# Opening and second batch of an attention-and-mixer kernel: feature widths, head halves, engines and slots changed

## Chip, core and metric

The kernel runs on one core of one Trainium2 chip. A core has TensorE (PE in the profile, with PEld for the loading of its weights), VectorE (DVE), ScalarE (ACT), GpSimd (POOL) and SyncE (SP), each with its own queue of instructions taken in order, and DMA queues filled by some of them. PE writes to PSUM, whose tiles here come from two pools. The metric is the device time of one execution in microseconds (us), compared as a median of runs.

## What is computed

Linear attention with cosine and sine weights of the position, and then a mixer over tokens and over channels. Shapes: batch B = 8, heads H = 8, sequence S = 576, head size D = 64, so a row has 512 columns after the heads are joined.

```python
def phi(x, c, s):
    r = np.maximum(x, 0.0)
    return np.concatenate([r * c, r * s], axis=-1)
q_p = phi(q, cos_w, sin_w)
k_p = phi(k, cos_w, sin_w)
kv = np.einsum('bhsf,bhsd->bhfd', k_p, v)
z = np.sum(k_p, axis=2)
num = np.einsum('bhsf,bhfd->bhsd', q_p, kv)
den = np.einsum('bhsf,bhf->bhs', q_p, z)[..., None] + 1e-06
x = num / den                       # heads joined: [B, 576, 512]
h = np.maximum(x.T @ w_tok1, 0.0) @ w_tok2      # over tokens: 576 -> 256 -> 576
u = x + h.T
h2 = np.maximum(u @ w_ch1, 0.0) @ w_ch2         # over channels: 512 -> 1536 -> 512
out = u + h2
```

## The kernel before

The sequence is cut into four blocks of 128 rows (0 to 3) and a tail of 64 rows that the code calls block R (R = 4); the tail holds four heads in each half of the partitions. The features of one block, cosine and sine side by side, have 128 columns for each head, so each head of a block is one 128x128 tile. For each batch there are two stages.

The **front** (class `Front`) makes u. `feature` (L210) computes relu and weight in one instruction on DVE (L227) or ACT (L225); `k_side` and `q_side` call it for cosine and sine. `ksum` (L239) adds up key features on PE, `ksum_out` copies the sums on ACT, `dens` multiplies query features by them. `q_trans` (L301) turns the query features of a block on PE, eight heads into one PSUM tile, and copies them out on ACT or DVE into `qpT`. `values` casts v into `v_aug`. `kv` (L273) multiplies keys by values into `kv_ps`, `kv_out` copies it to `kv_sb`. `num` (L320) multiplies turned queries by `kv_sb` and DVE divides into `x_sb`. `tok1`, `tok1_out` and `tok2` are the token mixer; `tok2` writes u with one addition on DVE for each block, `u_ps` being its PSUM tile.

The **channel** stage (class `Channel`) has 12 steps of the first product (`c_main`, with `c_tail` for the tail rows behind it) and then steps of the second (`o_step`, two matmuls of 512 columns each, for the first batch in 26 steps: the blocks 0 and 1 in turn, 12 steps; block 2, 6 steps; R, 2; block 3, 6). A finished block is added to u on DVE and stored by a DMA from SP.

The channel stage of a batch carries the front of the next one. `pieces` (L449) returns a plan, a slot number for each piece; slot C + n follows step n, slot O + n follows step 12 + n, and slot -1 comes before the first step. What a slot issues stands on each engine's queue behind the step, in the order of the plan. For the first batch the steps 0 to 2 are empty, since `first_front` has done their products. The second batch's u is turned by two transposing DMAs on SP (`u_trans_dma`, L421), which `c_main` of the second batch waits for. `tok2` of the first batch stands in slots too, for u is not needed until the first `o_step` ends.

The very first front (`first_front`, L593) has nothing to hide behind. It runs on loads that are cut into head halves: the low heads 0 to 3 of q, k and v come from one DMA each, the high heads from another; that of q's high heads is issued by ACT, all others by SP. Between its products stand fillers, `busy` (L184): matmuls of 512 columns of zeros into `idle_ps`, in PE's order like any other instruction. In this front u is made turned, straight from x and the token weights (`turned_x`, `turned_b`), and the first three steps of the channel product follow (`c_block`, L507).

PSUM: pool `ps_mm` has four buffers of one bank, pool `ps_at` two of two banks. The program gives a tile a buffer that is free in program order; the tile's first matmul then waits until the last reader of the buffer's earlier tile is done. All orders are written out by hand; the engines run in that order.

Loads of the later batches are issued by SP in `load_batch`: the second batch's behind the first channel weights, the third batch's behind the second channel weights.

Of the kernel before, what the change touches and what calls it, by code (L numbers as in the profile page):

```python
# [9 lines left out]
F32 = mybir.dt.float32  # L10
BF16 = mybir.dt.bfloat16
# [5 lines left out]
def kernel(  # L17
# [15 lines left out]
    nc = tc.nc  # L33

    B, H, S, D = q.shape
# [4 lines left out]
    P = 128  # L40
    R = S // P
    SM = R * P
    ST = S - SM
    NSC = R + 1
    NCC = Dm // P
    NT = D_tok // P
    NCH = D_ch // P
    HH = H // 2
# [8 lines left out]
    def half(g):  # L57
        return slice(g * ST, (g + 1) * ST)
# [12 lines left out]
    ps_mm = ctx.enter_context(tc.tile_pool(name="ps_mm", bufs=4, space=bass.MemoryType.PSUM))  # L71
    ps_at = ctx.enter_context(tc.tile_pool(name="ps_at", bufs=2, space=bass.MemoryType.PSUM))
# [111 lines left out]
    def busy(dst, times):  # L184
        for _i in range(times):
            nc.tensor.matmul(dst, ident, zeros[:, 0:dst.shape[-1]], start=True, stop=True)  # L186
# [10 lines left out]
    class Front:  # L197
# [100 lines left out]
                     self.kv_ps[g][:, 0:HH * DP]  # L298
                     .rearrange("p (j d) -> p j d", d=DP)[:, :, 0:D1])

        def q_trans(self, ci, heads=(0, H), eng=nc.scalar):  # L301
            lo, hi = heads if ci < R or self.padded else (0, HH)
            if hi - lo == H:
                qT_ps = ps_at.tile([P, H, P], BF16, name="qT_ps", tag="at")
            else:
                qT_ps = ps_mm.tile([P, HH, P], BF16, name="qT_ps", tag="mm")
            for h in range(lo, hi):
                nc.tensor.transpose(qT_ps[:, h - lo, :],  # L308
                                    self.qp[ci][:, h, :, :].rearrange("p a b -> p (a b)"), ident)
            dst = self.qpT[:, ci * H + lo:ci * H + hi, :]  # L310
            if eng is nc.scalar:
                nc.scalar.copy(dst, qT_ps)  # L312
            else:
                nc.vector.tensor_copy(dst, qT_ps)
# [3 lines left out]
                                        in_=self.qp[ci].rearrange("p h a b -> p (h a b)"))  # L318

        def num(self, ci, fill=0, dens=False):  # L320
            num_ps = ps_at.tile([P, 2, 512], F32, name="num_ps", tag="at")
            if fill:
                busy(num_ps[:, 0, HH * DP:512], 1)
            n = 2 if ci < R else 1
            for h in range(H):
                g, j = divmod(h, HH) if ci < R else (h % 2, h // 2)
                kv = self.kv_sb[g][:, j, 0:D1]
                cols = slice(j * DP, j * DP + D1)
                if ci < R:
                    nc.tensor.matmul(num_ps[:, g, cols], self.qpT[:, ci * H + h, :], kv,  # L330
                                     start=True, stop=True)
                elif self.padded:
                    nc.tensor.matmul(num_ps[:, 0, cols], self.qpT[:, R * H + g * HH + j, :], kv,
                                     start=(g == 0), stop=(g == 1))
                else:
                    nc.tensor.matmul(num_ps[half(g), 0, cols], self.qpT[:, R * H + j, half(g)], kv,
                                     start=True, stop=True)
            nv = num_ps[:, 0:n, 0:HH * DP].rearrange("p g (j d) -> p g j d", d=DP)
            if dens:
                den = self.d_sb[:, ci * H:ci * H + n * HH, :].rearrange("p (g j) o -> p g j o", g=n)  # L340
            else:
                den = small.tile([P, 2, HH, 1], F32, name="den")[:, 0:n]
                nc.vector.tensor_scalar_add(den, nv[:, :, :, D:D1], 1e-6)  # L343
                nc.vector.reciprocal(den, den)
            nc.vector.tensor_mul(  # L345
                self.x[:, ci, 0:n * DH].rearrange("p (g j d) -> p g j d", g=n, j=HH),
                nv[:, :, :, 0:D], den.to_broadcast([P, n, HH, D]))
# [101 lines left out]
        def pieces(self, first=False):  # L449


            V, KV, N = self.values, self.kv, self.num
            KS, QS, QT, T = self.k_side, self.q_side, self.q_trans, self.tok2
            C, O = 0, NCH
            if first:

                plan = [(C + at, KS, ci, 0 < ci < R) for ci, at in enumerate((3, 4, 5, 5, 6))]
                plan += [(C + at, QS, ci) for ci, at in enumerate((6, 7, 8, 8, 9))]
                plan += [(C + at, QT, ci, (0, H), nc.vector if ci == R else nc.scalar)
                         for ci, at in enumerate((9, 10, 11, 12, 13))]  # L460
                plan += [(C + at, V, ci, nc.vector) for ci, at in enumerate((10, 11, 11, 11, 11))]
                plan += [(O + at, KV, ci) for ci, at in enumerate((1, 1, 1, 2, 2))]
                plan.append((O + 2, self.kv_out, (0, 1), nc.vector))
            else:
                plan = [(C + at, V, ci, nc.scalar) for ci, at in enumerate((-1, -1, 0, 1, 2))]
                plan += [(C + at, KS, ci) for ci, at in enumerate((0, 0, 1, 2, 2))]
                for ci, at in zip(ORDER, (1, 2, 3, 4, 5)):
                    plan += [(C + at, QS, ci), (C + at, self.q_trans_dma, ci)]
                plan += [(C + at, KV, ci) for ci, at in enumerate((2, 3, 4, 6, 7))]
                plan.append((C + 8, self.kv_out))  # L470
            if first:
                at, mix, t = (O + 4, O + 6, O + 7, O + 9, O + 10), O + 11, O + 14
            else:
                at, mix, t = (C + 9, C + 10, C + 11, O + 1, O + 3), O + 4, O + 8
            plan += [(i, N, ci) for i, ci in zip(at, ORDER)]
            plan += [(mix, self.mix_head, 0), (mix + 1, self.mix_head, 1),
                     (mix + 2, self.mix_tail)]

            plan += [(t + at, T, ci) for ci, at in enumerate((0, 1, 2, 3, 3))]
            plan += [(t + 2, self.u_trans_dma, 0, 3), (t + 3, self.u_trans_dma, 3, NSC)]  # L480
            slots = {}
            for slot, what, *args in sorted(plan, key=lambda p: p[0]):
                slots.setdefault(slot, []).append((what, args))
            return slots


    AHEAD = 3
# [105 lines left out]
    def first_front(f):  # L593


        idle_ps = ps_at.tile([P, 2, 512], F32, name="idle_ps", tag="at")[:, 0, :]
        lo_heads, hi_heads = (0, HH), (HH, H)
        busy(idle_ps, 12)

        for j in range(2):  # L600
            f.feature("q", 3, j, lo_heads, on_act=True)
        for heads in (lo_heads, hi_heads):
            for ci in range(R):
                if (heads, ci) != (lo_heads, 3):
                    f.feature("q", ci, 0, heads)
                    f.feature("q", ci, 1, heads)
                f.q_trans(ci, heads)
                busy(idle_ps, 1)
        f.q_side(R)
        f.q_trans(R)  # L610
        busy(idle_ps, 2)
        for ci in range(R):
            f.feature("k", ci, 0)
            f.feature("k", ci, 1, on_act=(ci > 1))
            busy(idle_ps, 2)
            f.ksum(ci)
        f.k_side(R)
        busy(idle_ps, 2)
        f.ksum(R)
        busy(idle_ps, 1)  # L620
        for ci in range(R):
            if ci == 2:
                f.ksum_out()
            f.values(ci, nc.scalar, lo_heads)
        cast_tok1(0)
        f.values(R, nc.vector)
        for ci in range(R):
            f.values(ci, nc.vector, hi_heads)
        for ci in (0, 1, 2):
            f.dens(ci)  # L630
        for ci in range(NSC):
# [64 lines left out]
    w_ch2_done = load_w_ch2(done[1])  # L696
    f = Front(0, results[0])
    c = first_front(f)
    for b in range(B):
        slots = Front(b + 1, results[b + 1]).pieces(first=(b == 0)) if b + 1 < B else {}  # L700
        if b == 0:
            for ci in range(NSC):
                slots.setdefault(AHEAD + ci, []).insert(0, (f.tok2, (ci, ps_at, False)))
        if b > 0:
            c = Channel(b, results[b])
        for what, args in slots.pop(-1, ()):
            what(*args)
        for i, step in enumerate(c.steps(AHEAD if b == 0 else 0)):
            step()
            for what, args in slots.pop(i, ()):  # L710
                what(*args)


            if b == 0 and i == NCH:
                load_batch(2, "kvq", behind=w_ch2_done[1])
            if 0 < b < B - 2 and i == NSC:
                load_batch(b + 2, "vq")
            if b < B - 3 and i == NCH + (18 if b == 0 else 12):
                load_batch(b + 3, "k")
        assert not slots  # L720
# [32 lines left out]
```

## Time and profile before

| what | us |
|---|---|
| median of 3 runs | 274.07 (273.32 to 274.42) |
| the profiled execution, its own time | 273.47 |
| its span, first to last instruction | 271.7 |
| PE busy | 262.8 (97% of the span) |
| DVE busy | 165.4 (61%) |
| ACT busy | 123.8 (46%) |
| PE's first matmul of `c_block` (end of the first front) | 24.94 |
| last `o_step` matmul of the first batch ends, second batch's first product starts | 60.87, 61.81 |
| one batch in the middle, from `c_main` to `c_main` | 30.4 |

A row of the timeline reads: start in us, length in us, engine, line, operation, the tile written and the tiles read, shape, count of instructions merged into the row, and in brackets the idle time before it with what ended it. The length of a PE row runs to the end of its last matmul, which overlaps the next, so what a row costs PE is read from its start to the next start. A row of the waits reads: who waited, for whom, us in total, times, longest. Some records of matmuls can be missing from a trace.

### The profile page before, as it was taken

Reading aid. Unit: us, or ns where it says so; the run is one execution under the profiler, and the core shown is the slowest. Engines: PE = TensorE matmul, PEld = TensorE weight load, DVE = VectorE, ACT = ScalarE, POOL = GpSimd, SP = SyncE. Lnnn points to the kernel's source line nnn. Section 1 sums busy time; section 2 is a strip of 40 time slices with the busy share of each in tenths; the row PEclk is TensorE's granted clock in tenths of the full one; section 3 lists DMA queues with packets and bytes.
Section 4 is the critical chain, followed back from the end, with each engine's and each line's share of the span. In section 5 each row is a group of like instructions: output and inputs, shape, how many; then the busy total and the mean of one; then the engine's idle time right before and its main releaser. Section 6 shows DMA issues by size and latency. Waiting matters only on the chain.

```text
span 271.7 us, 5917 instructions
## 1 busy us (share of the span) xinstructions
PE 262.8 (97%) x2386; PEld 145.5 (54%) x2414; DVE 165.4 (61%) x421; ACT 123.8 (46%) x235; POOL 7.8 (3%) x21
## 2 busy tenths in 40 slices
PE   7989999999999999999999999999999999999994
PEld 2566466445555456455555455455555455454542
DVE  4954696759466495649666596639666586630031
ACT  4963882055616264236616264236625364315500
POOL 3400300000000000000000000000000000000000
PEclk9999999999999999999999999999999999999999
DMA  7999999959994889868696988769795453061022
GB/s 214 371 258 300 318 189 274 355 65 297 198 321 91 240 228 215 278 161 275 134 281 186 281 165 237 243 159 278 156 325 137 151 117 80 39 183 41 0 80 97
DMA packets 95483, 54.46 MB, mean 200 GB/s; under 512 B 62688, under 2 KB 90976, under 8 KB 95456
## 3 DMA queue, kind: packets, MB, share of 16 engines
q1 hardware_dynamic: 92016, 50.28, 66.7%
q0 software_dynamic: 2832, 3.21, 7.1%
q10 hardware_dynamic: 608, 0.59, 0.7%
q8 instruction: 19, 0.31, 0.5%
q14 instruction: 8, 0.07, 0.1%
HBM read 35.85 MB, written 9.44 MB: 167 GB/s over the span
## 4 chain that ended last, share of the span: by engine, by line
PE 92%; ACT 3%; DMA 2%; DVE 1%; issue 1%; POOL 0%; POOLq 0%; ACTq 0%
PE o_ps L535 29%; PE c_ps L501 29%; PE b_ps L358 5%; PE u_ps L386 4%; PE ct_ps L520 4%; PE kv_ps L287 4%; PE idle_ps L186 3%; PE o_ps L539 3%; PE num_ps L330 3%; DMA uT<-u_bf 2%; ACT qpT L312 1%; PE b_ps L362 1%; PE c_ps L511 1%; PE u_ps L390 1%; PE qT_ps L308 1%
## 5 line engine op out<-in xcount | busy, mean ns | idle before, releaser
L535 PE MATMUL o_ps<-w_ch,h1T 128*128 128x512 bf16 x367 | 94.1, 379 | 1.2
L501 PE MATMUL c_ps<-uT,w_ch 128*128 128x512 bf16 (+2 forms) x384 | 92.2, 372 | 1.0 <-DMA uT<-u_bf 0.9
L505 ACT ACTIVATE h1T<-c_ps 128x512 bf16<-128x512 f32 x93 | 55.7, 601 | 62.6 <-PE c_ps L501 62.4
L545 DVE TENSOR_TENSOR o_sb<-o_ps,u_sb 128x512 f32<-128x512 f32 (+1 forms) x40 | 25.4, 635 | 53.1 <-PE o_ps L535 49.6
L535 PEld LDWEIGHTS <-h1T 128*128 128x128 bf16 x384 | 35.1, 98 | 35.6 <-issue 1.6
L501 PEld LDWEIGHTS <-w_ch 128*128 128x128 bf16 x384 | 32.5, 97 | 29.2 <-DMA uT<-u_bf 1.4
L520 PEld LDWEIGHTS <-w_ch 128*128 128x128 bf16 x384 | 22.0, 98 | 18.4
L393 DVE TENSOR_TENSOR u_sb<-u_ps,x_sb 128x512 f32<-128x512 f32 (+1 forms) x40 | 24.7, 633 | 9.8 <-PE u_ps L386 9.5
L395 ACT CAST u_bf<-u_sb 128x512 bf16<-128x512 f32 (+1 forms) x35 | 19.4, 574 | 18.5 <-DVE u_sb L393 16.9
L520 PE MATMUL ct_ps<-uT,w_ch 128*128 128x64 bf16 x384 | 24.1, 193 | 0.0
L368 ACT ACTIVATE B<-b_ps 128x512 bf16<-128x512 f32 x8 | 4.8, 597 | 42.1 <-PE b_ps L358 42.1
L345 DVE TENSOR_TENSOR x_sb<-num_ps,den 128x512 bf16<-128x512 f32 (+1 forms) x35 | 22.3, 638 | 1.2
L227 DVE TENSOR_SCALAR qp<-qt,cos_t 128x512 bf16<-128x512 f32 (+1 forms) x50 | 20.4, 419 | 0.9 <-DMA qt<-in_q_dram 0.9
L227 DVE TENSOR_SCALAR qp<-qt,sin_t 128x512 bf16<-128x512 f32 (+1 forms) x50 | 20.4, 419 | 0.0
L227 DVE TENSOR_SCALAR kp<-kt,cos_t 128x512 bf16<-128x512 f32 (+1 forms) x47 | 20.0, 442 | 0.3 <-DMA kt<-in_k_dram 0.3
L235 ACT CAST v_aug<-vt 128x512 bf16<-128x512 f32 (+1 forms) x34 | 18.1, 556 | 0.0
L358 PE MATMUL b_ps<-x_sb,w_tok 128*128 128x512 bf16 x63 | 17.7, 379 | 0.1
L386 PE MATMUL u_ps<-B,w_tok 128*128 128x512 bf16 x57 | 17.6, 379 | 0.1
L227 DVE TENSOR_SCALAR kp<-kt,sin_t 128x512 bf16<-128x512 f32 (+1 forms) x42 | 17.5, 430 | 0.0
L343 DVE TENSOR_SCALAR den<-num_ps 128x8 f32<-128x8 f32 (+1 forms) x35 | 5.7, 164 | 18.3 <-PE num_ps L330 17.7
L287 PE MATMUL kv_ps<-v_aug,kp 128*128 128x65 bf16 (+1 forms) x320 | 15.5, 193 | 0.3 <-ACT qpT L312 0.3
L330 PE MATMUL num_ps<-kv_sb,qpT 128*128 128x65 bf16 x256 | 14.0, 193 | 0.7 <-DVE x_sb L345 0.5
(80 smaller groups left out, 186.3 us busy)
## 6 DMA issues: line engine op xcount, KB each, us to landing
out_dram<-o_sb SPq DMA_DIRECT2D x32, 256.0 KB, 3.7
kt<-in_k_dram SPq DMA_DIRECT2D x7, 1024.0 KB, 5.9
qt<-in_q_dram SPq DMA_DIRECT2D x7, 1024.0 KB, 7.9
vt<-in_v_dram SPq DMA_DIRECT2D x7, 1024.0 KB, 6.5
w_ch<-in_moe_w_ch_dram POOLq DMA_DIRECT2D x4, 384.0 KB, 9.8
w_ch<-in_moe_w_ch_dram POOLq DMA_DIRECT2D x3, 512.0 KB, 8.8
qt<-in_q_dram SPq DMA_DIRECT2D x16, 64.0 KB, 6.2
kt<-in_k_dram SPq DMA_DIRECT2D x2, 512.0 KB, 6.5
```

The lines of the kernel that those rows point to most:

```text
L227: nc.vector.tensor_scalar(o_ap, i_ap, scalar1=w, scalar2=0.0, op0=ALU.mult, op1=ALU.max)
L287: nc.tensor.matmul(self.kv_ps[g][:, j * DP:j * DP + D1], self.kp[ci][rows, i, :, :].rearrange("p a b -> p (a b)"), self.va[rows, ci, i if ...
L330: nc.tensor.matmul(num_ps[:, g, cols], self.qpT[:, ci * H + h, :], kv, start=True, stop=True)
L345: nc.vector.tensor_mul(self.x[:, ci, 0:n * DH].rearrange("p (g j d) -> p g j d", g=n, j=HH), nv[:, :, :, 0:D], den.to_broadcast([P, n, HH, ...
L358: nc.tensor.matmul(self.b1_ps[mi], w_tok1[:, ci, cols], self.x[:, ci, :], start=(ci == 0), stop=(ci == R - 1))
L386: nc.tensor.matmul(u_ps, w_tok2[:, ki, ci * P:(ci + 1) * P], self.B1[:, ki, :], start=(ki == 0), stop=(ki == NT - 1))
L393: nc.vector.tensor_add(res["u"][:, ci, 0:n], u_ps[:, 0:n], self.x[:, ci, 0:n])
L501: nc.tensor.matmul(c_ps[:, lo:hi], w_ch1[:, ki, mi * P:(mi + 1) * P], uT[:, lo // P:hi // P, ki, :], start=(ki == 0), stop=(ki == NCC - 1))
L505: nc.scalar.activation(self.h1T[:, mi, 0:SM], c_ps, AF.Relu)
L520: nc.tensor.matmul(self.ct_ps[:, mi % 6, :], w_ch1[:, ki, mi * P:(mi + 1) * P], self.res["uT"][:, R * NCC + ki % 2, half(ki // 2)], start= ...
L535: nc.tensor.matmul(o_ps, self.h1T[:, ki, ci * P:(ci + 1) * P], w_ch2[:, ki, :], start=start, stop=stop)
L545: nc.vector.tensor_add(o_sb[:, 0:n], o_ps[:, 0:n], res["u"][:, ci, 0:n])
```

## The change

In the first front, query features are made for all eight heads at once (512 columns), in the block order 0, 1, 3, 2, R, with block 3's on ACT; each block's eight transposes go into one tile of `ps_mm`, copied out at once, with two fillers behind each. Key features are made in head halves, low heads of all blocks and then high heads; the key sums follow the halves, with two fillers ahead of each low group, one ahead of each of the first three high groups, and none ahead of the tail's. Values are shared out: low heads of blocks 0 and 1 and high heads of 2 and 3 on ACT, the tail, low heads of 2 and 3 and high heads of 0 and 1 on DVE. The key sums' copy stands behind ACT's first two value casts. `num` of block R, in this front, takes its PSUM tile from `ps_mm`.

In the second batch's front, features, transposes, values and kv come up to two slots sooner (the features and kv), the copies of the transposes alternate between ACT and DVE in place of ACT four times and DVE once, `kv_out` is on ACT in place of DVE, and `num`, the token mixer and `u_trans_dma` come one slot sooner. `tok2` of the first batch moves from slots 3 to 7 to slots -1, -1, 11, 12 and 13, behind the other pieces of its slot.

```diff
-        def q_trans(self, ci, heads=(0, H), eng=nc.scalar):
-            lo, hi = heads if ci < R or self.padded else (0, HH)
-            if hi - lo == H:
-                qT_ps = ps_at.tile([P, H, P], BF16, name="qT_ps", tag="at")
-            else:
-                qT_ps = ps_mm.tile([P, HH, P], BF16, name="qT_ps", tag="mm")
-            for h in range(lo, hi):
-                nc.tensor.transpose(qT_ps[:, h - lo, :],
+        def q_trans(self, ci, eng=nc.scalar, pool=ps_at):
+            lo, hi = 0, H if ci < R or self.padded else HH
+            qT_ps = pool.tile([P, hi, P], BF16, name="qT_ps", tag=("at" if pool is ps_at else "mm"))
+            for h in range(hi):
+                nc.tensor.transpose(qT_ps[:, h, :],
...
         def num(self, ci, fill=0, dens=False):
-            num_ps = ps_at.tile([P, 2, 512], F32, name="num_ps", tag="at")
+            if dens and ci == R:
+                num_ps = ps_mm.tile([P, 1, 512], F32, name="num_ps", tag="mm")
+            else:
+                num_ps = ps_at.tile([P, 2, 512], F32, name="num_ps", tag="at")
...
-                plan = [(C + at, KS, ci, 0 < ci < R) for ci, at in enumerate((3, 4, 5, 5, 6))]
-                plan += [(C + at, QS, ci) for ci, at in enumerate((6, 7, 8, 8, 9))]
-                plan += [(C + at, QT, ci, (0, H), nc.vector if ci == R else nc.scalar)
-                         for ci, at in enumerate((9, 10, 11, 12, 13))]
-                plan += [(C + at, V, ci, nc.vector) for ci, at in enumerate((10, 11, 11, 11, 11))]
-                plan += [(O + at, KV, ci) for ci, at in enumerate((1, 1, 1, 2, 2))]
-                plan.append((O + 2, self.kv_out, (0, 1), nc.vector))
+                plan = [(C + at, KS, ci, 0 < ci < R) for ci, at in enumerate((3, 3, 4, 4, 5))]
+                plan += [(C + at, QS, ci) for ci, at in enumerate((5, 6, 6, 7, 7))]
+                plan += [(C + at, QT, ci, nc.vector if ci % 2 else nc.scalar)
+                         for ci, at in enumerate((7, 8, 9, 9, 10))]
+                plan += [(C + at, V, ci, nc.vector) for ci, at in enumerate((9, 9, 9, 10, 10))]
+                plan += [(C + at, KV, ci) for ci, at in enumerate((11, 11, 11, 12, 12))]
+                plan.append((O, self.kv_out))
...
-                at, mix, t = (O + 4, O + 6, O + 7, O + 9, O + 10), O + 11, O + 14
+                at, mix, t = (O + 3, O + 5, O + 6, O + 8, O + 9), O + 10, O + 13
...
-        for j in range(2):
-            f.feature("q", 3, j, lo_heads, on_act=True)
-        for heads in (lo_heads, hi_heads):
-            for ci in range(R):
-                if (heads, ci) != (lo_heads, 3):
-                    f.feature("q", ci, 0, heads)
-                    f.feature("q", ci, 1, heads)
-                f.q_trans(ci, heads)
+        f.feature("q", 3, 0, on_act=True)
+        f.feature("q", 3, 1, on_act=True)
+        for ci in (0, 1, 3, 2, R):
+            if ci != 3:
+                f.q_side(ci)
+            f.q_trans(ci, pool=ps_mm)
+            busy(idle_ps, 2)
+        for ci in range(R):
+            f.feature("k", ci, 0, lo_heads)
+            f.feature("k", ci, 1, lo_heads)
+            busy(idle_ps, 2)
+            f.ksum(ci, lo_heads)
+        for ci in range(R):
+            f.feature("k", ci, 0, hi_heads)
+            f.feature("k", ci, 1, hi_heads, on_act=(ci > 1))
+            if ci < 3:
                 busy(idle_ps, 1)
-        f.q_side(R)
-        f.q_trans(R)
-        busy(idle_ps, 2)
+            f.ksum(ci, hi_heads)
+        f.k_side(R)
+        f.ksum(R)
+        for ci in (0, 1):
+            f.values(ci, nc.scalar, lo_heads)
+        f.ksum_out()
+        f.values(R, nc.vector)
+        for ci in (2, 3):
+            f.values(ci, nc.vector, lo_heads)
         for ci in range(R):
-            f.feature("k", ci, 0)
-            f.feature("k", ci, 1, on_act=(ci > 1))
-            busy(idle_ps, 2)
-            f.ksum(ci)
-        f.k_side(R)
-        busy(idle_ps, 2)
-        f.ksum(R)
-        busy(idle_ps, 1)
-        for ci in range(R):
-            if ci == 2:
-                f.ksum_out()
-            f.values(ci, nc.scalar, lo_heads)
+            f.values(ci, nc.vector if ci < 2 else nc.scalar, hi_heads)
         cast_tok1(0)
-        f.values(R, nc.vector)
-        for ci in range(R):
-            f.values(ci, nc.vector, hi_heads)
...
-            for ci in range(NSC):
-                slots.setdefault(AHEAD + ci, []).insert(0, (f.tok2, (ci, ps_at, False)))
+            for ci, at in enumerate((-1, -1, NCH - 1, NCH, NCH + 1)):
+                slots.setdefault(at, []).append((f.tok2, (ci, ps_at, False)))
```

## The prediction

> **What bounds the kernel now.** I read the page first: TensorE (PE) is busy 97% of the 271.7 us span, and the chain that ended last is 92% PE. So the time is the sum of PE's work plus PE's waits, and a part of the change is worth what it adds to or takes from PE's order. The diff leaves PE's arithmetic from the second batch's channel stage on alone; it can act only in the opening (0 to 24.94 us, where the first `c_block` starts), in the first batch's channel stage that carries the second batch's front (to 60.87), and in the one wait behind that. Next the timeline of PE in the opening, around the key sums:
>
> ```profile
> 6.46 0.40 PE L308 MATMUL qT_ps<-ident,qp 128*128 128x128 bf16 x4
> 6.70 0.38 PE L186 MATMUL idle_ps<-zeros,ident 128*128 128x512 bf16 x1
> ...
> 12.15 0.35 PE L246 MATMUL ks_ps<-ones,kp 128*128 128x1 bf16 x8
> 12.37 0.59 PE L186 MATMUL idle_ps<-zeros,ident 128*128 128x512 bf16 x2
> 12.80 0.34 PE L246 MATMUL ks_ps<-ones,kp 128*128 128x1 bf16 x8
> 13.00 0.59 PE L186 MATMUL idle_ps<-zeros,ident 128*128 128x512 bf16 x2
> 13.43 0.34 PE L246 MATMUL ks_ps<-ones,kp 128*128 128x1 bf16 x8
> 13.63 0.59 PE L186 MATMUL idle_ps<-zeros,ident 128*128 128x512 bf16 x2
> 14.06 0.34 PE L246 MATMUL ks_ps<-ones,kp 128*128 128x1 bf16 x8
> ```
>
> From start to start: eight key sums take 0.22, two filler matmuls 0.43 (0.216 each), four transposes 0.22. From 12.37 on there is no gap: the fillers, not VectorE (DVE), set when the last key sum starts (14.06). DVE's timeline has its last key feature there:
>
> ```profile
> 5.79 0.35 DVE L227 TENSOR_SCALAR qp<-qt,cos_t 128x256 bf16<-128x256 f32 x1 [0.88 <-DMA qt<-in_q_dram]
> 6.06 0.35 DVE L227 TENSOR_SCALAR qp<-qt,sin_t 128x256 bf16<-128x256 f32 x1
> ...
> 11.22 0.48 DVE L227 TENSOR_SCALAR kp<-kt,cos_t 128x512 bf16<-128x512 f32 x1
> 11.62 0.48 DVE L227 TENSOR_SCALAR kp<-kt,sin_t 128x512 bf16<-128x512 f32 x1
> ...
> 13.07 0.34 DVE L227 TENSOR_SCALAR kp<-kt,sin_t 128x256 bf16<-128x256 f32 x1
> ```
>
> A feature of 256 columns costs 0.262 from start to start, one of 512 columns 0.40. The last ends at 13.41, 0.65 before PE gets to it. Landings of the first loads, asked of the DMA view by short stretches (us at the end of the row, from issue):
>
> ```profile
> qt<-in_q_dram SPq DMA_DIRECT2D x1, 512.0 KB, 5.0
> qt<-in_q_dram ACTq DMA_DIRECT2D x1, 512.0 KB, 5.6
> ```
>
> Issued at 0.75 and 0.76, the low heads of q land at 5.75 and the high heads at 6.36. Last, the chain at the end of the first batch, and the waits up to 62 us:
>
> ```profile
> 57.07 4.69 DMA uT<-u_bf
> 61.81 2.79 PE c_ps L501 x24
> ```
>
> ```profile
> PE c_ps L501 <- DMA uT<-u_bf: 0.9, 1, 0.9
> PE kv_ps L287 <- ACT qpT L312: 0.3, 1, 0.3
> ```
>
> PE runs out of work at 60.87 and waits 0.94 for the transposed u of the second batch. Of the other waits between 25 and 61.8 us only one is large: 0.31 at 42.2, where the kv product waits for ScalarE's (ACT's) copy of transposed queries. All PE idle in that stretch is 36.80 - 35.16 = 1.64.
>
> **Part 1, the opening up to the key sums.** q features become 512 wide, so the first waits for both halves: 6.40 on DVE in place of 5.79. Block 0 is ready at 6.40 + 0.40 + 0.48 = 7.28, and PE's first transpose starts at 7.33 in place of 6.46. PE then owes, up to the start of the last key sum: 36 transposes, 36 / 4 x 0.22 = 1.98; ten fillers among them, 2.16; low key heads, 4 x (0.43 + 0.11) = 2.16; high key heads, 3 x 0.216 + 4 x 0.11 = 1.09. Together 7.39: the last key sum starts at 14.72. Does another engine hold it up more? DVE: six 512-wide (2.37) and two 256-wide q features (0.52) end at 9.29, behind the low heads of k (issued 2.71, landed 6.0 later, 8.7); then eight, six and two 256-wide key features, 16 x 0.262 = 4.19, the last written at 13.57. ACT: two 512-wide q features from 6.42 at 0.71, four copies of 1024 columns at 0.93 and one of 512 at 0.48, then two key features at 0.51: 13.2. Both are before PE's 14.6 to 14.7. Splitting keys costs DVE 1.3 more, but under PE. So the queries that DVE finishes 0.7 sooner are paid by PE's later start: before, PE had 0.44 of waits between 6.46 and 14.06 that the late start eats, and one more filler is in the way. Cost **+0.66**. Bounds: -0.45 if PE's fillers did not count (DVE's 13.57 plus 0.04 against 14.06), +0.87 if PE's whole later start came through.
>
> **Values on both engines, key sums out.** ACT reads the key sums at 15.1, and has its two low value halves (0.3 each) done by 13.9; DVE does R, two low and two high halves from 13.48 to 14.6 (0.205 each); ACT's two high halves end near 15.9. PE needs the low ones at 15.3 + 0.6 = 15.9 and the high ones at 17.2. Nothing; the cover is the key sums' lateness, and if PE were early it would be 0.3 at most.
>
> **`num` of block R in the other PSUM pool.** Before, its first matmul stood at 19.67 though PE's previous one ended at 19.57, and block 3 followed at 20.36. A buffer more takes that 0.10 out: **-0.10** (bounds 0 and -0.14). What follows is moved as a whole: `c_block` at 24.94 + 0.56. ACT's casts of the token weights wait for landings at 15.3 and 18.3, both now passed by then.
>
> **Part 2, the second batch's front in the slots.** In the old frame (add 0.56), PE starts with u of blocks 0 and 1 at 27.53 (0.43 each), then steps 3 to 9 at 0.98 (3 has 0.12 more), transposes of queries 0 and 1 (0.44 each): it comes to the transposes of blocks 2 and 3 at 36.27 and 36.72. The latter take the PSUM buffer of block 1, whose copy is now on DVE, and DVE has in its queue ahead of it: u 0 and 1 (ready 28.16, 0.61 each), five 512-wide key features and four 256-wide (3.05), eight and four query features (4.21): 36.64. This row gives the copy:
>
> ```profile
> 42.25 0.69 DVE L314 COPY qpT<-qT_ps 128x1024 bf16<-128x1024 bf16 x1 [0.62 <-PE qT_ps L308]
> ```
>
> It ends at 37.33, so PE waits until 37.38: **+0.66**. Queued behind it on PE are step 10 and everything later; on DVE the values, which end at 40.1 under kv at 40.5. The old wait at 42.2 goes, **-0.31**: kv's buffer comes from block 3's copy, done at 38.6. `kv_out` goes from DVE (0.77) to ACT (0.38 twice), read by `num` only three slots on. u of block 3 takes the buffer that is free longest, that of u 2, whose addition ends at 42.5 as PE arrives: nothing (bounds 0 and +0.85, a rival). u of block 4 takes kv's buffer at 43.4, as `kv_out` ends. Features are in no danger from loads: k of the second batch lands by 28.4, q by 32.4, v by 35.6 on the clock of the trace, DVE wants them at 29.9, 33.0 and 39.
>
> **`num`, mix and T one slot sooner.** Their spacing stays; so do their small waits. T's two transposing DMAs go ahead of one more slot, whose own work is two o matmuls: 0.43 more of PE's work lies behind the first DMA, and 0.94 becomes 0.51: **-0.43** (bounds 0 and -0.94). On SP's queue the second transpose now stands before the store of block 2 in place of after it, which only helps; the loads of the second next batch hang on the channel weights' landing (41.12) and not on PE, and end by 55. POOL's queue is passed by nothing.
>
> **Sum:** 0.66 - 0.10 + 0.66 - 0.31 - 0.43 = **+0.48 us**. The profiled execution took 273.47 (1.77 around its span); it becomes 273.95. It lies 0.60 under the median of 274.07, so the median becomes **274.55**, given as 274.5. A measurement of this kernel can tell about 0.5% (1.37 us) from no change: this is no change.
>
> **Rivals.**
> (a) *The opening is not PE's, and the rest works as meant.* DVE sets the key sums (-0.45), -0.10, both waits in the slots go (-0.31, +0), the uT wait goes whole (-0.94): -1.80, **272.3**. For it: fillers are short and DVE's order is rearranged throughout. Against: PE's rows from 12.37 on without a gap.
> (b) *The clock.* The twelve first fillers start 0.427 apart up to 6.04, and every later one 0.216: PE ran at half speed for its first 5.1 us. The change puts a hole of 0.87 (6.46 to 7.33) just there. If the rise starts over, 5.1 us from 7.33 run at half speed and cost half of it, 2.55, in a stretch that PE sets: +3.03, **277.1**. It decides from 1.8 us of half speed on (0.48 + 0.9 passes 1.37). Against: the step to 0.216 had come before the hole, the old trace had holes of 0.07 there and one of 0.12 later and stayed fast, and its granted clock column is 9 throughout, so shows nothing of it. [...]
> (c) *u 3 takes kv's buffer* and waits for `kv_out` on ACT: 0.69 of copies and some 0.16 of handing over, +0.85, **275.4**. Against: in the opening, block 0's `num` started (17.30) before the second `kv_out` (17.41), so it took the buffer free longer.
> (d) *The slot buys nothing:* the first transposing DMA took 4.7 to landing where later batches show 2.9 to 3.2; were its end tied to something else than its issue, the 0.43 stays away: **275.0**. Against: it was issued at 57.07, right behind its last cast.
>
> **Chances.** Forecast 0.46 (its own range 273.7 to 275.4, from the bounds of part 1 and of the uT wait), (a) 0.17, (b) 0.17, (c) 0.12, (d) 0.08. Faster: most of (a), 0.15. Slower: (b), half of (c) and a tail of the forecast, 0.26. Same: 0.59. The range goes from (a)'s 272.3, less a little, to a (b) with 4.1 us at half speed in place of 5.1 (0.48 + 2.05): 272.4 to 276.6.
>
> **What would show it.** First transposes of `qT_ps` near 7.3; the last `ks_ps` group starting near 14.7, behind `idle_ps` without a gap, while DVE's last key feature ends near 13.6; `c_block` near 25.5; a PE wait of some 0.7 at the fourth `qT_ps` of the second batch, named DVE qpT; no PE wait at kv; the uT wait near 0.5. Wrong if fillers stand 0.43 apart after 7.3 (b), if the key sums wait for DVE (a), or if u 3 waits for ACT (c).

## The result, and the profile after

| | median us | lowest to highest | runs |
|---|---|---|---|
| before | 273.77 | 273.24 to 274.81 | 14 |
| after | 276.03 | 274.45 to 278.40 | 14 |

The ratio is 1.0077 (95% interval 1.005 to 1.0103): 0.8% slower, where no change was forecast. The median lies in the prediction's wide range of 272.4 to 276.6, but above the forecast's own 273.7 to 275.4. The spread says more than the median. Before, all runs lie within 1.6 us; after, within 4. Put in order of the mean granted clock of each run, the runs after fall apart:

| mean granted clock | runs | us |
|---|---|---|
| 0.997 to 1.000 | 7 | 274.45 to 276.24, median 274.99 |
| 0.993, 0.994 | 2 | 278.40, 275.25 |
| 0.985 to 0.988 | 5 | 276.48 to 277.02, median 276.78 |

Of 100 runs of the kernel before that stood beside the experiments, 99 had 0.997 or more, one 0.994. So the change has two costs to explain: 1.2 us in the runs at full clock (274.99 against 273.77), and some 1.8 us more in 5 of 14 runs that lose clock. The profiled execution of after took 274.84 at a clock of 1.000; it shows the first cost only.

Its chain of waits, shares by engine, was 92% PE and 2% DMA before:

```profile
PE 81%; DMA 14%; POOL 2%; SPq 2%; issue 0%; DVE 0%; ACT 0%; ACTq 0%
```

PE's timeline of after, at the places that the prediction named:

```profile
6.98 0.62 PE L305 MATMUL qT_ps<-ident,qp 128*128 128x128 bf16 x8 [1.16 <-DVE qp L227]
...
13.93 0.38 PE L186 MATMUL idle_ps<-zeros,ident 128*128 128x512 bf16 x1
14.14 0.54 PE L246 MATMUL ks_ps<-ones,kp 128*128 128x1 bf16 x16
14.94 0.74 PE L266 MATMUL d_ps<-ks_sb,qpT 128*128 128x1 bf16 x24 [0.25 <-ACT ks_sb L254]
15.54 0.87 PE L287 MATMUL kv_ps<-v_aug,kp 128*128 128x65 bf16 x20
16.34 0.57 PE L266 MATMUL d_ps<-ks_sb,qpT 128*64 128x1 bf16 x16
16.77 0.87 PE L287 MATMUL kv_ps<-v_aug,kp 128*128 128x65 bf16 x20
17.58 0.26 PE L186 MATMUL num_ps<-zeros,ident 128*128 128x192 bf16 x1
...
25.22 2.75 PE L511 MATMUL c_ps<-uT,w_ch 128*128 128x512 bf16 x12
...
37.63 0.61 PE L305 MATMUL qT_ps<-ident,qp 128*128 128x128 bf16 x8 [0.47 <-DVE qpT L311]
...
42.40 0.59 PE L535 MATMUL o_ps<-w_ch,h1T 128*128 128x512 bf16 x2 [0.37 <-DMA w_ch<-in_moe_w_ch_dram]
...
63.13 1.15 PE L501 MATMUL c_ps<-uT,w_ch 128*128 128x384 bf16 x6 [1.17 <-DMA uT<-u_bf]
```

The reader is to see three things. The opening loses 0.28 (`c_block` at 25.22, 24.94 before). At 42.40 there is a wait that before did not have, for channel weights. The wait for the turned u is 1.17, not 0.51. At 63.13 the second batch's first product is 1.32 behind its place before (61.81), which is nearly all of the 1.37 between the two profiled executions.

Where the channel weights are late shows in GpSimd's (POOL's) own rows, of before and then of after. L169 issues the four loads of the first channel weights, L175 the three of the second:

```profile
10.61 3.15 POOL L169 DMA_DIRECT2D w_ch<-in_moe_w_ch_dram  x4 [7.33 <-DMA kt<-in_k_dram]
31.41 2.24 POOL L175 DMA_DIRECT2D w_ch<-in_moe_w_ch_dram  x3 [17.65 <-DMA qt<-in_q_dram]
```

```profile
9.86 6.68 POOL L169 DMA_DIRECT2D w_ch<-in_moe_w_ch_dram  x4 [6.58 <-DMA kt<-in_k_dram]
32.63 6.14 POOL L175 DMA_DIRECT2D w_ch<-in_moe_w_ch_dram  x3 [16.08 <-DMA qt<-in_q_dram]
```

The same seven instructions take 12.8 us in place of 5.4. Taken one by one, the loss is in the first of each group: 4.53 (9.86 to 14.39) and 4.65 (32.63 to 37.28), while all others after, and all seven before, take 0.72 to 0.84. VectorE's rows of after in these two stretches:

```profile
12.88 0.35 DVE L227 TENSOR_SCALAR kp<-kt,sin_t 128x256 bf16<-128x256 f32 x1
13.15 1.10 DVE L237 CAST v_aug<-vt 128x256 bf16<-128x256 f32 x5
16.95 0.20 DVE L270 TENSOR_SCALAR d_sb<-d_ps 128x36 f32<-128x36 f32 x1 [2.70 <-PE d_ps L266]
...
32.15 0.61 DVE L227 TENSOR_SCALAR kp<-kt,sin_t 128x256 bf16<-128x256 f32 x2
...
35.84 0.61 DVE L227 TENSOR_SCALAR qp<-qt,cos_t 128x256 bf16<-128x256 f32 x2
36.37 0.61 DVE L227 TENSOR_SCALAR qp<-qt,sin_t 128x256 bf16<-128x256 f32 x2
36.89 0.68 DVE L311 COPY qpT<-qT_ps 128x1024 bf16<-128x1024 bf16 x1
```

VectorE works without a gap up to 14.25 and, on features, up to 36.98; GpSimd's issue ends 0.14 and 0.30 behind these. What hangs on it is the third batch's loads on SP, of before and of after:

```profile
41.12 0.37 SPq L85 DMA_DIRECT2D kt<-in_k_dram  x1
```

```profile
45.25 0.37 SPq L85 DMA_DIRECT2D kt<-in_k_dram  x1
```

They move 4.13 later, next to the transposing DMA of u. The chain of after reads it in one piece, from q's landing over GpSimd and the weights to PE, and later from u's cast to its landing:

```profile
23.26 9.08 DMA qt<-in_q_dram
32.34 0.29 issue
32.63 9.73 DMA w_ch<-in_moe_w_ch_dram
42.40 0.59 PE o_ps L535 x2
```

```profile
57.00 0.51 DVE u_sb L393
57.50 5.58 DMA uT<-u_bf
63.08 0.04 issue
63.13 2.79 PE c_ps L501 x24
```

### The profile page after: what moved, and what is told of

Same layout as the page of the kernel before. It is cut to its first block, busy times and chain, and to the rows that moved or that the text cites. A ratio compares the mean times of both kernels' runs of the same rounds, so it can differ in the third digit from the quotient of the medians.

```text
span 273.0 us, 5940 instructions
## 1 busy us (share of the span) xinstructions
PE 263.6 (97%) x2414; PEld 145.3 (53%) x2414; DVE 165.1 (60%) x420; ACT 123.0 (45%) x232; POOL 15.3 (6%) x21
## 4 chain that ended last, share of the span: by engine, by line
PE 81%; DMA 14%; POOL 2%; SPq 2%; issue 0%; DVE 0%; ACT 0%; ACTq 0%
PE o_ps L535 29%; PE c_ps L501 27%; DMA w_ch<-in_moe_w_ch_dram 6%; PE u_ps L386 5%; PE b_ps L358 4%; PE ct_ps L520 4%; PE o_ps L539 3%; DMA qt<-in_q_dram 3%; PE num_ps L330 3%; PE kv_ps L287 3%; DMA kt<-in_k_dram 2%; DMA uT<-u_bf 2%; POOL w_ch L169 2%; PE b_ps L362 1%; SPq L90 1%; PE u_ps L390 1%
## 5 line engine op out<-in xcount | busy, mean ns | idle before, releaser
L535 PE MATMUL o_ps<-w_ch,h1T 128*128 128x512 bf16 x384 | 95.5, 379 | 0.4 <-DMA w_ch<-in_moe_w_ch_dram 0.4
L227 DVE TENSOR_SCALAR qp<-qt,cos_t 128x512 bf16<-128x512 f32 (+1 forms) x46 | 19.5, 437 | 1.1 <-DMA qt<-in_q_dram 1.1
L227 DVE TENSOR_SCALAR qp<-qt,sin_t 128x512 bf16<-128x512 f32 (+1 forms) x46 | 19.5, 437 | 0.0
L386 PE MATMUL u_ps<-B,w_tok 128*128 128x512 bf16 x64 | 19.0, 379 | 0.1
L227 DVE TENSOR_SCALAR kp<-kt,sin_t 128x512 bf16<-128x512 f32 (+1 forms) x46 | 18.8, 421 | 0.0
```

Of the source, the lines that this page charges most:

```text
L227: nc.vector.tensor_scalar(o_ap, i_ap, scalar1=w, scalar2=0.0, op0=ALU.mult, op1=ALU.max)
L386: nc.tensor.matmul(u_ps, w_tok2[:, ki, ci * P:(ci + 1) * P], self.B1[:, ki, :], start=(ki == 0), stop=(ki == NT - 1))
L535: nc.tensor.matmul(o_ps, self.h1T[:, ki, ci * P:(ci + 1) * P], w_ch2[:, ki, :], start=start, stop=stop)
```

## The experiments

Two theories stood behind them. **The held issue:** features that come sooner fall where GpSimd wants to issue weights; beside VectorE's run of instructions the issue lasts to about the run's end (4.53 and 4.65 us in after), and the loads behind it are late. **The clock:** some runs lose granted clock in the opening; at first the hole ahead of the first transposes (the prediction's rival b) was suspected. Every kernel was run in five rounds beside the kernel before, whose medians were 273.86, 273.86, 273.68 and 273.68 in the four groups below. "Dropped" are runs with a mean granted clock of 0.984 to 0.988.

### First group: the parts alone, the hole, the weights

**open_alone:** the opening of after, all slots as before (the second part of the diff taken back).

> The opening of the changed kernel with the slots of the one before. [...] Clock theory (the hole between the first fillers and the first transposes lets PE's clock fall in some executions): the whole loss and spread of the changed kernel are here, median +1.5 to +2.5 us, runs spread over 3 us or more, mean granted clock near 0.986 in the long ones.

**slots_alone:** the opening of before, all slots as after (the first part taken back).

> The opening of before with the slots of the changed kernel. [...] Clock theory: no hole, so no spread: clock 1.000 in all runs, time within 0.5 us of before.

**no_hole:** after, with four more fillers in the hole at the first transposes.

```diff
-        busy(idle_ps, 12)
+        busy(idle_ps, 16)
```

> The changed kernel with 16 first fillers in place of 12, so that PE has no hole of 1.2 us ahead of the first transposes. Clock theory: the spread goes (1.5 us or less), clock 1.000 in all runs, median near 274.5 to 275. [...]

**w2_early:** after, with the second channel weights released by the landing of k, not of q, so that GpSimd issues them some 2 us sooner.

```diff
-    w_ch2_done = load_w_ch2(done[1])
+    w_ch2_done = load_w_ch2(done[0])
```

> The changed kernel with the second weights' load behind the keys of the second batch in place of its queries, so that GpSimd issues it near 29.1, while VectorE adds u from PSUM. [...] Clock theory: median and spread of the changed kernel stay.

| | median us | ratio (interval) | dropped | median of runs at 0.996 or more |
|---|---|---|---|---|
| open_alone | 274.48 | 1.0043 (1.0014 to 1.0072) | 5 of 12 | 273.98 |
| slots_alone | 274.68 | 1.0037 (1.0015 to 1.0059) | 0 of 12 | 274.49 |
| no_hole | 276.81 | 1.0103 (1.0081 to 1.0125) | 5 of 6 | none |
| w2_early | 274.27 | 1.0026 (1.0006 to 1.0045) | 2 of 12 | 274.20 |

So the clock goes with the opening and the steady loss with the slots: at full clock open_alone is 0.1 above the kernel before, slots_alone 0.6. In slots_alone the first issue of the second weights takes 4.83, in open_alone 0.86. (Two runs of slots_alone, 275.22 and 277.10, had a clock of 0.994.)

The hole is refuted as the place: with it cut from 1.16 to 0.45 five of six runs dropped (the sixth, the profiled one, had 0.994). A profile that caught the drop shows where it is. Stretches of open_alone; the columns are the stretch, its length, busy us of PE, PEld, DVE, ACT and POOL with counts, the granted clock, DMA and GB/s:

```profile
16.00:17.00 1.00, 1.00 (x35) 0.88 (x31) 0.00 (x0) 0.57 (x2) 0.79 (x2) 1.00 0.85 66
17.00:18.00 1.00, 1.00 (x30) 0.90 (x27) 0.57 (x2) 0.15 (x2) 0.00 (x0) 0.95 1.09 198
18.00:19.00 1.00, 0.98 (x17) 0.87 (x16) 0.22 (x1) 1.00 (x3) 0.00 (x0) 0.50 1.16 207
...
23.00:24.00 1.00, 1.00 (x5) 0.56 (x4) 0.47 (x1) 0.00 (x0) 0.00 (x0) 0.50 1.16 217
24.00:25.00 1.00, 1.00 (x7) 0.52 (x5) 0.00 (x0) 0.10 (x1) 0.00 (x0) 0.63 1.03 268
25.00:26.00 1.00, 1.00 (x18) 0.95 (x17) 0.69 (x1) 0.50 (x1) 0.00 (x0) 1.00 1.01 315
```

PE counts as fully busy, and yet the clock falls to a half at 17.90 and comes back at 24.73. The records of the granted clock give 17.90 and 24.73 there, 18.23 and 21.65 in no_hole: 6.83 and 3.42 us, and each drop lies whole multiples of 3.41 behind the first rise (4.25 and 4.58). In before and after the record at full clock is 266.24 and 269.65 us long, 78 and 79 times 3.413. One such step at half speed takes 0.5 x 3.41 / 273 = 0.006 off the mean clock and two take 0.0125: these are the groups at 0.994 and 0.987. What stands ahead of the drop is what the change made of the tail's key sums: it took away three fillers, two ahead of them and one behind. From 14.14 to 17.58 PE then has only matmuls of 1 and 65 columns, 3.44 us, where before such a stretch ran from about 14.5 to 17.3 (its filler behind the sums has no record; the load of the filler's weights stands at 14.24). The new clock theory: a step filled with such narrow matmuls has a drop behind it.

In w2_early the weights' issue is short again (2.62 us for the three, 6.14 in after), and the transposing DMA of u has little beside it. GpSimd's row, then the stretch around the issue of the transposing DMA, w2_early first, after second:

```profile
30.30 2.62 POOL L175 DMA_DIRECT2D w_ch<-in_moe_w_ch_dram  x3 [13.76 <-DMA kt<-in_k_dram]
```

```profile
57.00:59.00 2.00, 2.00 (x26) 1.23 (x26) 1.70 (x4) 1.64 (x4) 0.00 (x0) 1.00 0.04 15
```

```profile
57.00:59.00 2.00, 2.00 (x30) 1.37 (x28) 1.62 (x3) 1.75 (x4) 0.00 (x0) 1.00 0.96 324
```

```profile
PE qT_ps L305 <- DVE qpT L311: 0.5, 1, 0.5
PE qT_ps L305 <- DVE qp L227: 0.5, 1, 0.5
PE c_ps L501 <- DMA uT<-u_bf: 0.5, 1, 0.5
```

The last fence is PE's waits from 25 to 64 us in w2_early. The queue is all but empty (15 GB/s against 324), the transposing DMA takes 4.92 in place of 5.58, and the wait is the 0.51 that the prediction had worked out. No wait for weights is left; that for q features (the second row) is new, VectorE having stood 0.32 for k ahead of its features.

The held issue is not simply an issue that comes into a run of VectorE. In w2_early it starts at 30.30, when features have run since 30.03. In no_hole, whose slots and weights are those of after, it starts at 32.59, 3 us into a run without a gap, and takes 0.81:

```profile
32.59 2.36 POOL L175 DMA_DIRECT2D w_ch<-in_moe_w_ch_dram  x3 [16.39 <-DMA qt<-in_q_dram]
31.55 1.93 DVE L227 TENSOR_SCALAR kp<-kt,cos_t 128x512 bf16<-128x512 f32 x5
```

There the wait for weights is gone too, and the wait for u is 0.70. What the profiles of all kernels share is the width of the feature that VectorE is in when the first issue starts: 15 first issues that started in a feature of 256 columns took 3.2 to 5.5, 13 that started in one of 512, in an addition or in none took 0.76 to 0.92. Both of after started in one of 256 (9.86 and 32.63), that of no_hole's second weights in one of 512 (its row above merges three of 512, the third from 32.34, with two of 256). No run changed the width alone, so this is a rule that fits and not a cause shown.

### Second group: fillers back, and taken from before

**filler_back:** after, with one filler behind the tail's key sums.

```diff
         f.k_side(R)
         f.ksum(R)
+        busy(idle_ps, 1)
```

> The changed kernel with one filler matmul put back behind the tail's key sums, where PE waits 0.25 us for ScalarE anyway. In two profiles that fell in slow runs the granted clock dropped to 0.5 at 17.90 and 18.23 us, at the end of a 3.41 us window that began just behind the last filler and held only matmuls of 1 and 65 columns; in a third, not slow, the window began 0.9 us behind it. Window theory: with this filler no such window is left, mean clock 0.994 or more in every run, median 274.6 to 275.2, range 2 us or less. Rival (the hole ahead of the first transposes does it): clocks of 0.985 to 0.988 in a third of the runs, median near 276 as before.

**before_thin:** the kernel before, without its three fillers there.

```diff
-        busy(idle_ps, 2)
         f.ksum(R)
-        busy(idle_ps, 1)
```

> The kernel before without its three fillers around the tail's key sums (two ahead, one behind). Window theory: PE gets there 0.4 us sooner, and the fast runs are 0.2 to 0.5 us faster than before, but a fifth to a half of the runs show a clock of 0.985 to 0.988 and take 2 to 3 us more, which before never does. Rival (the hole): no run with such a clock; all 0.2 to 0.5 us faster.

**both_mended:** filler_back and w2_early together.

> The changed kernel with the filler put back and the second weights' load behind the second batch's keys. [...]

**all_mended:** both_mended, one filler behind each block's transposes instead of two, and block 1's transposes copied by ACT instead of DVE.

```diff
-                plan += [(C + at, QT, ci, nc.vector if ci % 2 else nc.scalar)
+                plan += [(C + at, QT, ci, nc.vector if ci == 3 else nc.scalar)
...
             f.q_trans(ci, pool=ps_mm)
-            busy(idle_ps, 2)
+            busy(idle_ps, 1)
```

> As the last, and with one filler in place of two behind each block of transposed queries in the opening (five fillers, 1.08 us of PE's order), and the second batch's query block 1 copied by ScalarE in place of VectorE. If PE's order of fillers sets the opening, the last key sums start 0.6 to 1.0 us sooner, near 13.4 to 13.6, then bound by VectorE's features; the wait of 0.5 at the second batch's fourth transposes goes; together 272.8 to 273.4, below before. If VectorE's features set the opening, only the 0.5 goes: 273.6 or more. If the thinner fillers let the clock fall: runs with 0.986 and 2 us more.

| | median us | ratio (interval) | dropped | median of runs at 0.996 or more |
|---|---|---|---|---|
| filler_back | 274.58 | 1.0040 (1.0022 to 1.0059) | 0 of 11 | 274.57 |
| before_thin | 275.33 | 1.0025 (0.9997 to 1.0054) | 6 of 11 | 273.24 |
| both_mended | 274.65 | 1.0046 (1.0024 to 1.0068) | 3 of 12 | 274.39 |
| all_mended | 272.45 | 0.9954 (0.9936 to 0.9973) | 0 of 7 | 272.45 |

A twelfth run of before_thin took 552.15 at a clock of 1.000 and is not in the last two columns; its cause is open. The median counts it, that of the other eleven is 275.03.

before_thin is the cleanest proof of the clock: three instructions that compute nothing are taken out of a kernel that otherwise is the one before, and 6 of 11 runs drop, to a median of 275.68, while the others run 0.6 faster than before. Its profiled execution:

```profile
16.00:17.00 1.00, 1.00 (x33) 0.88 (x30) 0.11 (x1) 0.69 (x2) 0.00 (x0) 0.95 1.15 227
17.00:18.00 1.00, 1.00 (x17) 0.82 (x15) 0.47 (x2) 0.00 (x1) 0.00 (x0) 0.50 1.15 221
```

This drop comes at 16.90. The step of 3.41 us ahead of it, from 13.49, does hold fillers of 512 columns, and so does that of all_again (fourth group), 13.52 to 16.93. One line of each:

```profile
13.65 0.59 PE L186 MATMUL idle_ps<-zeros,ident 128*128 128x512 bf16 x2
13.85 0.38 PE L186 MATMUL idle_ps<-zeros,ident 128*128 128x512 bf16 x1
```

And two steps without any, in after from 15.06 to 18.47 and in three_fillers from 15.75 to 19.16, counted from their first rises (4.82 and 5.51), were followed by no drop. So "only narrow matmuls" is not the rule. An estimate does part the steps of all profiles: the columns of the matmuls that fall into each step, added up from the timelines (before's filler without a record included). The four steps ahead of the drops in the opening hold some 2780 to 3290 columns, the one ahead of filler_back's (below) some 2160, and every step at full clock that was followed by none some 3430 or more; fillers alone, at 0.216 each, would fill one with some 8100. The margin is small, and no run was made to test it.

One filler helps, but both_mended's three dropped runs (276.13 to 276.48) refute the expectation of filler_back that one is enough.

filler_back shows how the held issue can cost clock too. In its profile the second weights' first issue took 5.51, PE had nothing from 61.9 to 64.2, and the clock fell behind that:

```profile
62.00:64.00 2.00, 0.00 (x0) 0.00 (x0) 2.00 (x5) 0.00 (x0) 0.00 (x0) 1.00 0.59 129
64.00:66.00 2.00, 1.77 (x6) 0.85 (x7) 2.00 (x6) 0.00 (x0) 0.00 (x0) 0.59 1.13 286
```

That run took 277.63 at a mean clock of 0.994. All runs of 277 us or more at 0.993 and above, in all groups, are of kernels with the late issue (before_thin's 552.15 apart).

all_mended is faster than both kernels. Its timeline of PE at the tail's key sums:

```profile
12.99 0.34 PE L246 MATMUL ks_ps<-ones,kp 128*128 128x1 bf16 x8
13.49 0.35 PE L246 MATMUL ks_ps<-ones,kp 128*128 128x1 bf16 x8 [0.16 <-DVE kp L227]
13.71 0.38 PE L186 MATMUL idle_ps<-zeros,ident 128*128 128x512 bf16 x1
```

With five fillers less among the transposes PE comes to the last sums early, and they wait 0.16 for VectorE: the opening is then VectorE's, if barely, and `c_block` starts at 24.38. Of the waits from 25 to 64 us only one of 0.3 is left, at the transposes. The wait for u is gone in part because the first transposing DMA took 3.5 to landing here, 4.9 in w2_early; why it did is open.

### Third group: the fillers of before in after

**three_fillers:** after, with the three fillers as before (two ahead of the tail's sums, one behind).

> The changed kernel with before's three fillers around the tail's key sums (two ahead, one behind), the second weights' load as changed. [...] If fillers do not decide: a quarter or more of the runs at 0.985 to 0.988.

**three_fillers_w2:** the same with the weights early.

> The same with the second weights' load behind the second batch's keys. Window theory: clock 0.997 or more in every run, range 1.5 us or less, and only what is left of the opening (c_block 0.5 to 0.7 us later) less the uT wait gained (0.4): 274.1 to 274.6. [...] If fillers do not decide: three or more of some twelve runs at 0.985 to 0.988, as with one filler.

| | median us | lowest to highest | ratio (interval) | dropped |
|---|---|---|---|---|
| three_fillers | 275.20 | 274.46 to 277.58 | 1.0063 (1.0034 to 1.0092) | 0 of 9 |
| three_fillers_w2 | 274.67 | 274.26 to 275.65 | 1.0036 (1.0018 to 1.0053) | 0 of 12 |

With the fillers of before no run falls to 0.988 (one of each kernel is at 0.994, 277.58 and 275.65), and with the weights early the spread falls from 3.1 to 1.4 us. The issue's own share is 0.5 of the medians; in the profiles the wait for u is 2.3 and 0.49. The fillers cost their time: `c_block` at 25.66, 0.44 after the kernel after.

### Fourth group: the best one again

**all_again:** all_mended unchanged. **all_three:** all_mended with all three fillers.

> The kernel all_mended once more. Is its gain the same, and does one filler hold the clock in it? In the changed opening with one filler 3 of 23 runs fell to 0.986 so far. If one filler is not enough here either: one or two of some ten runs at 0.985 to 0.988 and about 274.5 us; the others 272.0 to 272.8 as before. If it is: all of them there.

> all_mended with before's three fillers around the tail's key sums. The two ahead of them take 0.43 us of PE's order, of which 0.16 to 0.3 lie in a wait for VectorE's last features: 0.1 to 0.3 us over all_mended, 272.5 to 272.9, clock 0.997 or more in every run.

| | median us | lowest to highest | ratio (interval) | dropped |
|---|---|---|---|---|
| all_again | 272.51 | 271.52 to 274.61 | 0.9961 (0.9936 to 0.9986) | 1 of 12 |
| all_three | 273.11 | 272.54 to 276.36 | 0.9984 (0.9962 to 1.0007) | 0 of 12 |

The repeat gives the same 0.4% gain. One run dropped (274.61, 0.987; its profile has the drop at 16.93); two more had 0.992 and 0.994. With two more fillers none of 12 dropped, which one of 19 without them does not let one tell from chance, and the median is 0.6 higher. Not all of that need be the fillers: in the profiles `c_block` is 0.43 later than in all_mended, and the first transposing DMA takes 4.9 in place of 3.5, with a wait of 0.49 behind it. Runs of all_again of 274.27 and 274.58 at clocks of 0.998 and 1.000, and one of all_three at 276.36, have no profile; their cause is open.

Pooled, for the changed opening: no filler behind the tail's sums, 17 of 44 runs dropped (after, open_alone, no_hole, w2_early); one filler, 4 of 42; three, 0 of 33. That none is worse than one or three is clear; one against three is not. The 12 runs at 0.992 to 0.994, one step by the sum above, are not in these counts: one is of the 100 runs of before, two each of after, slots_alone and all_again. Two have a profile: no_hole's drop lies in the opening, filler_back's behind the wait for u.

## Where the prediction was right and where it went wrong

**The step that failed** is in the second part: the loads of the second next batch "hang on the channel weights' landing (41.12) and not on PE, and end by 55. POOL's queue is passed by nothing". The dependency was right, and 41.12 was taken as fixed. The landing hung on GpSimd's issue, which is long where it starts beside certain features of VectorE (4.65 in after, 0.76 to 0.92 elsewhere), and these the change moved onto it (in four of the five profiles that have the changed slots and the weights as changed; not in no_hole). The uT term came out as +0.23 in place of -0.43, and a wait of 0.37 for weights was new: together 1.03 beyond what was worked out. The profiled execution came out 0.89 over its forecast of 273.95; the opening (-0.28) and the transposes (-0.19) were cheaper than forecast, and 0.33 lies in spacings of PE that no wait names. That the held issue is the cause is shown by w2_early: with it gone the wait is 0.5 and no other part of the change was touched. Why an issue lasts long beside VectorE's run is not shown; the traces give the times alone. In after it ends 0.14 and 0.30 behind the run, after 4.53 and 4.65 us, and no_hole's issue beside such a run was short (0.81). Had rows of before been looked at for this, they warn only faintly: GpSimd's issue at 10.61 started beside features of 512 columns and was not held (its four took 0.73 to 0.84 each).

```profile
10.42 0.48 DVE L227 TENSOR_SCALAR kp<-kt,cos_t 128x512 bf16<-128x512 f32 x1 [0.34 <-DMA kt<-in_k_dram]
```

**The clock, rival (b)**, had the kind right: half speed. That its 277.1 is near the 276.78 of after's dropped runs is in part luck: it put 2.55 on the lost clock, where 1.8 was lost (276.78 - 274.99), and the rest of the distance to before is the 1.2 of the runs at full clock, which (b) did not have. Its place was wrong. The hole from 6.46 to 7.33 that it priced is not what does it (no_hole); what does it is the removal of fillers at 14 us, which the opening's working counted only as PE time saved. The condition "decides from 1.8 us of half speed" held in the runs that dropped: a drop lasts 3.41 or 6.83. In after itself no profile caught a drop; drops are shown in open_alone, no_hole, before_thin and all_again, and after's five runs have the same mean clock. No run shows the 4.1 us at half speed from which the range's upper end, 276.6, is worked out: the drops are one step of 3.41 or two. And the profile of open_alone calls PE 82% to 100% busy in the step ahead of its drop, with matmuls of 1 and 65 columns.

**Opening, +0.66:** 0.28 with num of R in it (0.56 was forecast). The mechanism was right: fillers and sums stand back to back from 10.73 to 14.14, and from the first transpose to the last sums (8 of the 16 at 14.14, so about 14.36) PE took 7.38, where 7.39 was worked out. Mis-sized was the start: q's high heads landed at 5.98, not 6.36, so the transposes start at 6.98, not 7.33. all_mended shows the other side of the claim that PE's fillers set it: five fillers less, and PE waits 0.16 for VectorE.

**num of R, -0.10:** 0. The three products of `num` keep their spacing (19.18 to 20.63, 1.45 us, against 1.46 before); the other pool released nothing.

**Transposes, +0.66 and -0.31:** 0.47, named VectorE's copy as forecast, and the wait at kv is gone. (The transposes of blocks 3 and R come three slots sooner, not two.)

**Rivals (a), (c), (d)** fell. (a): neither the opening nor u came sooner. (c): u of block 3 started before ACT's `kv_out` (43.52), with no wait named for it. (d): w2_early shows that the slot is worth its 0.43 once the loads are out of the way.

**The sum.** At full clock the parts alone cost 0.1 (opening) and 0.6 (slots), together 0.7, and the whole change 1.2; that the two are worse together than apart by 0.5 stays open. The rest of the median, up to 276.03, is the runs that lost clock. That it still lies in the stated range is luck in part: the range reaches up there only for (b), whose place was wrong, and the late weights were in none of its terms.

## What to carry to other kernels

Before moving VectorE work, look at which DMA issues of GpSimd it will stand beside, and which features they will meet: the issues held here all started in a feature of 256 columns, and one changed dependency, which released the second weights some 2 us sooner, took their delay away. A filler is to be priced by what it does to the clock as well as by its time: taking three out of the narrowest stretch saved 0.6 us and cost 2.4 in 6 of 11 runs. And where a kernel's runs spread, sort them by granted clock before explaining a median.

## What the runs showed of the hardware that was not expected

- The granted clock fell to 0.50 while the profile called PE busy (82% to 100% in open_alone), behind a step of 3.41 us that is mostly matmuls of 1 and 65 columns: at 17.90, 18.23, 16.90 and 16.93 us in four profiles, for one or two steps. By the estimate above such a step holds at most some 3290 columns. Beside transposes and 512-column fillers in turn (6.98 to 10.73 in after) the clock stayed at 1.00.
- In filler_back a drop at 64.36, back at 67.77, again 3.41, stood behind a wait of PE of 2.3 us (61.9 to 64.2; the load of its weights waited 2.8 for the transposing DMA). In three_fillers a wait of 2.29 (to 64.77) was followed by none. By an estimate from its first rise, 5.51 + 17 x 3.413, a border between two steps lies in that wait, at 63.53, and filler_back's wait lies in one step; that this decides is not shown.
- A first issue of weights by GpSimd took 3.2 to 5.5 us when it started beside a VectorE feature of 256 columns, and 0.76 to 0.92 otherwise; the issues behind it were not held (0.72 to 0.93).
- The first transposing DMA took 4.69 to landing in before and 4.92 in w2_early with the queues all but empty, but 3.5 and 3.4 in all_mended and all_again; what decides this is open.
